# A second drain of GpSimd in the last turn but one of a routed-attention and expert kernel

## The chip, the cores and the metric

The kernel runs on one core of one Trainium2 chip. A core has five engines with an instruction stream each: TensorE (PE, with its weight loads as PEld), VectorE (DVE), ScalarE (ACT), GpSimd (POOL) and SyncE (SP). They meet through semaphores. The metric is the device time of one execution in microseconds, and a kernel's time is the median of several executions.

## What is computed

There are two blocks, one behind the other. The first is attention in which a query attends only to the keys of its own cluster: `q`, `k` and `v` are 4 x 8 x 768 x 64, and each head has 16 centroids.

```python
q_assign = argmax(q_n @ c_n);  k_assign = argmax(k_n @ c_n)
mask = q_assign[:, :, :, None] == k_assign[:, :, None, :]
attn = softmax(where(mask, q @ k.T / sqrt(64), -1e9));  x = attn @ v
```

The result is seen as 3072 tokens (rows) of 512 columns. The second block sends each token to one of 8 experts, the one with the largest logit, and weighs the expert's answer by the softmax probability of that expert:

```python
e = argmax(x @ w_gate);  gate = softmax(x @ w_gate)[e]
y = gate * (relu(x @ w1[e]) @ w2[e])        # w1: 512 x 1024, w2: 1024 x 512
```

All is float32. No token is dropped, so the number of tokens of an expert follows from the data.

## The kernel before

**Attention.** Sixteen pairs of heads are worked through in turn: scores on TensorE, exponentials on ScalarE, sums on VectorE. The finished rows are stored to a DRAM buffer, `x_rows`. For each of the four batches `number(b)` works out a place for every token in a DRAM list sorted by expert, and writes the list with GpSimd: six indirect DMAs per batch (L541), 24 in all.

**Turns.** The expert block then runs in ten turns, `s` = 0 to 9. A turn takes up to a fixed number of tokens of one expert: 288 and 288 in the two early turns, then 256, 288, 288, 384, 416, 416, 448 and 128. The expert of a turn is read at run time from a small table. For each turn GpSimd gathers the token rows, 128 at a time, with indirect DMAs (`gather`, L672, 30 in all). VectorE weighs and transposes them, `layer1` multiplies by `w1`, `layer2` by `w2`, and `write` (L976 and L977) scatters each finished tile of up to 128 rows to `out` with one indirect DMA of GpSimd (30 in all). A finished tile is in a `z` buffer, of which there are three.

**The order of the work.** The schedule is written by hand: each engine's instructions run in the order in which the Python code emits them. Work for later turns is put between the steps of the present one with hooks: `at(h1, i, f, ...)` has `f` called at the i-th hook of the turn's first layer, `at(h2, i, f, ...)` at the i-th of the second. `layer1` has a hook behind each of its seven products in each of two halves, so that hook 4 comes in the first half, behind the fifth product. In turn 8 (448 tokens) that hook calls one sum of `w2` blocks for VectorE. Turn 8 has no gather of its own to issue, because `s + 2` is beyond the last turn; what stands in GpSimd's stream from there on is the four scatters of turn 8 and the one of turn 9.

**The end.** Behind the last turn each engine reads a flag (L1173) and branches over a general path that these inputs don't need (L1174). Then the program is closed on leaving the context of L1435, where SP waits for the outstanding semaphores in turn, every engine runs a drain instruction and they meet at a barrier. That code is not in the kernel's text; the drain of GpSimd in it is the first in its stream since the start of the program, where another stands (L1426).

Of the kernel before, what the change touches and what calls it, by code (L numbers as in the profile page):

```python
# [33 lines left out]
def kernel(  # L34
# [11 lines left out]
    nc = tc.nc  # L46
# [116 lines left out]
    with tc.manual_schedule(), ExitStack() as actx:  # L163
# [476 lines left out]
        def places(s):  # L640
            g = GR[s]
            off = nc.sync.value_load(xe[0:1, NS + s : NS + s + 1], min_val=0, max_val=(E - 1) * NPL + N)
            T = g["T"]
            full, rem = divmod(T, P)
            sf = g["sf"] = xp.tile([P, NJ, TR], F32, name="sf", bufs=4)
            nc.sync.dma_start(
                out=sf[:, 0:full, :], in_=t_d[bass.ds(off, full * P), :].rearrange("(j p) o -> p j o", p=P)
            )
            if rem:
                nc.sync.dma_start(out=sf[0:rem, full, :], in_=t_d[bass.ds(off + full * P, rem), :])  # L650
# [48 lines left out]
        def take(s):  # L699

            g = GR[s]
            T, C = g["T"], g["C"]
            g["xs"] = xp.tile([P, T_MAX // Q4, P], F32, name="xs")
            for r in range(HP):
                nc.sync.dma_start(
                    out=g["xs"][Q4 * r : Q4 * (r + 1), 0:C, :],
                    in_=g_d[s][0:T, P * r : P * (r + 1)].rearrange("(c t) d -> t c d", t=Q4),
                )
# [60 lines left out]
        for b in range(B - 1):  # L769
            n = HP * (b + 1)  # L770
            last = b == B - 2
# [56 lines left out]
    with tc.manual_schedule(), ExitStack() as ectx:  # L828
# [125 lines left out]
        def pairs_of(s):  # L954


            return GR[s]["T"] // (2 * P) if s else 0

        def h_sums(s):

            g = GR[s]
            g["H"] = []
            for p in range(pairs_of(s)):
                c0 = 2 * P * p
                h = g["h"]
                a11, a21 = h[:, 0:4, c0 : c0 + P], h[:, 0:4, c0 + P : c0 + 2 * P]
                a12, a22 = h[:, 4:8, c0 : c0 + P], h[:, 4:8, c0 + P : c0 + 2 * P]
                t = [hpool.tile([P, 4, P], F32, name=f"hs{i}") for i in range(4)]
                V = nc.vector
                strassen(V, t[2], a11, a21, ALU.subtract)  # L970
                strassen(V, t[0], a21, a22, ALU.add)
                strassen(V, t[1], t[0], a11, ALU.subtract)
                strassen(V, t[3], a12, t[1], ALU.subtract)
                g["H"].append((a11, a12, a22, t))
# [113 lines left out]
        last = NS - 1  # L1088

        def first_weights(s):  # L1090
            if s >= len(EARLY):
                expert(s)
            GR[s]["w1"] = fetch1(GR[s]["e"], (wa, wb)[s % 2])

        def second_weights(s):
            GR[s]["w2"] = fetch2(GR[s]["e"], (wa, wb)[s % 2])

        for s in range(NS):
            h1, h2 = {}, {}

            def at(d, i, f, *a):
                d.setdefault(i, []).append(lambda: f(*a))

            if s == 0:
                at(h1, 2, sum_up, n - 1)
                at(h1, 2, weights_of, n - 1)
                at(h1, 3, gate, B - 1)
                at(h1, 3, gate_exp, B - 1)
                at(h1, 5, gate_sum, B - 1)
                at(h1, 5, choose, B - 1)  # L1110
                at(h1, 8, count, B - 1)
                at(h1, 9, number, B - 1)
                at(h1, 11, rows, n - 1)
                at(h1, 11, store, n - 1)
                at(h1, 12, rank_all)
                at(h2, 0, rank_rest)
                at(h2, 3, places, 2)
                at(h2, 7, indices, 2)
                at(h2, 7, gather, 2)
            if s == 3:  # L1120
                at(h1, 5, ask)
                at(h1, 9, answer)
            if s < last:
                if 2 < s + 2 <= last:
                    places(s + 2)
                if s == 0:
                    first_weights(1)
                elif s > 1:
                    take(s + 1)
                if s == 1:  # L1130
                    at(h1, 6, weigh, 2)
                    at(h1, 7, take, 2)

                    at(h1, 7, first_weights, 2)
                    at(h1, 8, second_weights, 2)
                else:
                    second_weights(s + 1)
                if 0 < s <= last - 2:
                    at(h2, 0, first_weights, s + 2)

                if s == 0:
                    when = ((h2, 1), (h2, 2), (h2, 4), (h2, 5), (h2, 7), (h2, 7))
                elif s == 1:
                    when = ((h2, 2), (h2, 3), (h2, 4), (h2, 5), (h2, 6), (h2, 6))
                else:
                    when = ((h1, 9), (h1, 10), (h2, 1), (h2, 2), (h2, 2), (h2, 5))
                if GR[s + 1]["T"] >= 2 * P:
                    for (h, i), f, a in zip(when, (w1_sums,) * 4 + (w2_sums,) * 2, (2, 1, 0, 3, 2, 0)):
                        at(h, i, f, s + 1, (a,), nc.vector)
                at(h2, 1 if s == 1 else 3, turn_rows, s + 1)  # L1150
                if GR[s + 1]["T"] >= 2 * P:
                    at(h2, 1 if s == 1 else 4, x_sums, s + 1)
            if s == 0:
                at(h1, 2, gather, 1)
                at(h1, 8, weigh, 1, slice(0, 1))
                at(h1, 11, weigh, 1, slice(1, 2))
                at(h1, 12, weigh, 1, slice(2, 3))
                at(h1, 12, take, 1)
            elif s + 2 <= last:
                at(h1, 5 if s == 2 else 4, indices, s + 2)  # L1160
                at(h1, 5 if s == 2 else 4, gather, s + 2)
                at(h2, 6 if s == 1 else 4, weigh, s + 2)
            if pairs_of(s):
                at(h1, 4, w2_sums, s, (1,), nc.vector)
                at(h1, 6, w2_sums, s, (3,), nc.vector)
            (layer1 if GR[s]["T"] >= 2 * P else few_columns)(s, h1)
            h_sums(s)
            layer2(s, h2)
# [271 lines left out]
```

## Time and profile before

| what | value |
| --- | --- |
| median of 3 runs | 679.32 us (677.63 to 682.28) |
| the profiled execution's own time | 680.02 us |
| its span in the profile | 678.2 us |
| TensorE busy | 648.1 us, 96% of the span |
| VectorE, ScalarE busy | 512.5 and 301.0 us |
| GpSimd busy, instructions | 124.4 us, 145 |
| indirect DMAs of GpSimd | 84 (24 at L541, 30 at L672, 30 at L977) |

The profile is of one execution, whose time is the span and 1.8 us that lie outside it. All times inside it count from the start of the span. Instructions that the sequencer handles alone, such as branches, semaphore waits and drains, don't count as busy; they are found under the line that they belong to, with a q behind the engine's name (POOLq, SPq). A GpSimd DMA's duration is the time of its issue, not that of its data. The time that the page puts down as idle before an instruction is time of that engine, and costs something only where the end depends on it.

### The profile page before, as it was taken

The numbers are of one execution on the slowest core, as the hardware profiler recorded it, in microseconds if no ns is written. First come the engines' busy times: TensorE is split into PE (matmuls) and PEld (weight loads), VectorE is DVE, ScalarE is ACT, GpSimd is POOL, SyncE is SP. The second block draws the span as 40 slices with busy tenths as digits, with TensorE's granted clock in tenths as the row PEclk, the third lists the DMA queues.
The fourth block names the chain that finished last, engine by engine and source line by source line (L and its number), as shares of the span: only waits on it lengthen the run. The fifth ranks groups of instructions, "written<-read, shape, count | busy, mean of one in ns | idle before, by whom it ended". The sixth has DMA issues, their size and how long they took to land.

```text
span 678.2 us, 11364 instructions
## 1 busy us (share of the span) xinstructions
PE 648.1 (96%) x4210; PEld 424.3 (63%) x4210; DVE 512.5 (76%) x909; ACT 301.0 (44%) x524; POOL 124.4 (18%) x145
## 2 busy tenths in 40 slices
PE   4999999999999999999999989999999999999993
PEld 2445444455444454444484879978797977869771
DVE  5889999999999999999887788886868375562300
ACT  2756556667556566556432323333231332413210
POOL 4000000012000300222113522324241422040010
PEclk9899999999999999999999989999999999999997
DMA  9723455433455434356473498667494837523010
GB/s 185 144 51 73 88 94 94 67 70 69 80 94 94 73 73 78 63 152 197 113 264 96 147 388 281 227 261 251 196 288 175 271 127 218 201 73 135 7 49 17
DMA packets 191807, 95.37 MB, mean 141 GB/s; under 512 B 155967, under 2 KB 173887, under 8 KB 190464
## 3 DMA queue, kind: packets, MB, share of 16 engines
q1 hardware_dynamic: 184016, 81.12, 43.8%
q0 software_dynamic: 4928, 12.97, 5.8%
q10 hardware_dynamic: 2800, 0.48, 0.4%
q8 instruction: 35, 0.57, 0.4%
q14 instruction: 28, 0.23, 0.1%
HBM read 74.10 MB, written 20.70 MB: 140 GB/s over the span
## 4 chain that ended last, share of the span: by engine, by line
PE 52%; issue 27%; DVE 8%; DMA 5%; POOL 5%; SPq 2%; ACT 1%; POOLq 0%; DVEq 0%; ACTq 0%
PE sps L370 19%; PE mps L395 15%; PE bank L902 4%; PE bank L1003 3%; PE sbank L902 3%; POOL out_dram L977 3%; PE sbank L1003 2%; PE mps L415 2%; PE bank L1022 2%; PE mps L304 2%; DVE acc L389 2%; POOL xg L672 1%; DMA w<-in_moe_w_dram 1%; DVE a L723 1%; DVE xw L689 1%
## 5 line engine op out<-in xcount | busy, mean ns | idle before, releaser
L383 ACT ACTIVATE A<-sps 128x768 f32<-128x768 f32 x192 | 153.1, 811 | 47.3 <-PE sps L370 46.2
L370 PE MATMUL sps<-qT,kT 64*128 64x384 f32 x768 | 160.2, 496 | 1.9 <-ACT A L383 1.9
L389 DVE TENSOR_TENSOR acc<-acc,A 128x768 f32<-128x768 f32 x128 | 121.4, 948 | 9.7 <-ACT A L383 3.3
L395 PE MATMUL mps<-A,v_in 128*64 128x384 f32 x768 | 127.4, 488 | 0.0
L370 PEld LDWEIGHTS sps<-qT,kT 64*128 64x128 f32 x768 | 66.8, 188 | 57.8 <-issue 51.0
L395 PEld LDWEIGHTS mps<-A,v_in 128*64 128x64 f32 x768 | 53.8, 137 | 70.5 <-issue 62.2
L977 POOL DMA_INDIRECT out_dram<-z,si x30 | 47.8, 1594 | 199.9 <-DVE z L860 170.7
L541 POOL DMA_INDIRECT tokens_of<-tg,pos_i x24 | 27.1, 1128 | 291.8 <-DVE pos_i L539 145.8
L370 PE MATMUL sps<-mq,mk 64*128 64x384 bf16 x384 | 63.4, 324 | 2.7 <-ACT mq L350 2.7
L1022 PE MATMUL bank<-w,h 128*128 128x512 f32 (+2 forms) x224 | 64.4, 596 | 0.0
L672 POOL DMA_INDIRECT xg<-x_rows,gi x30 | 41.4, 1382 | 50.7 <-DVE gi L662 19.3
L350 ACT COPY mq<-ohT 32x384 bf16<-32x384 bf16 x64 | 32.6, 510 | 38.7 <-DVE ohT L340 29.5
L902 PE MATMUL sbank<-xc,a 128*128 128x144 f32 (+4 forms) x288 | 48.0, 310 | 1.4 <-ACT h L920 0.7
L902 PE MATMUL bank<-xT,w 128*128 128x144 f32 (+4 forms) x288 | 47.8, 309 | 0.0
L902 PEld LDWEIGHTS bank<-xT,w 128*128 128x128 f32 x288 | 43.9, 191 | 2.6 <-issue 2.2
L1022 PEld LDWEIGHTS bank<-w,h 128*128 128x128 f32 (+2 forms) x224 | 24.6, 151 | 32.5 <-issue 32.3
L902 PEld LDWEIGHTS sbank<-xc,a 128*128 128x128 f32 x288 | 43.3, 190 | 2.1 <-issue 1.2
L860 DVE TENSOR_TENSOR h<-sbank,p 128x288 f32<-128x288 f32 (+4 forms) x18 | 9.2, 513 | 46.8 <-PE sbank L902 45.7
L370 PEld LDWEIGHTS <-mk 64*128 64x128 bf16 x384 | 19.5, 94 | 28.2 <-DVE mk L352 3.3
L920 ACT ACTIVATE h<-h 128x288 f32<-128x288 f32 (+4 forms) x36 | 17.6, 488 | 41.4 <-DVE h L860 32.6
L689 DVE TENSOR_TENSOR xw<-xg,sf 128x256 f32<-128x256 f32 (+2 forms) x60 | 32.8, 607 | 2.2 <-DMA xg<-x_rows,gi 1.7
L389 DVE TENSOR_TENSOR acc<-A 128x768 f32<-128x768 f32 x32 | 30.3, 947 | 5.1 <-ACT A L383 5.0
(205 smaller groups left out, 884.5 us busy)
## 6 DMA issues: line engine op xcount, KB each, us to landing
w<-in_moe_w_dram SPq DMA_DIRECT2D x20, 2048.0 KB
v_in<-in_v_dram SPq DMA_DIRECT2D x32, 192.0 KB
x_rows<-x SPq DMA_DIRECT2D x64, 96.0 KB
turn_rows<-xw SPq DMA_DIRECT2D x23, 256.0 KB
q_in<-in_q_dram SPq DMA_DIRECT2D x60, 96.0 KB
k_in<-in_k_dram SPq DMA_DIRECT2D x60, 96.0 KB
xs<-turn_rows SPq DMA_DIRECT2D x16, 144.0 KB
xs<-turn_rows SPq DMA_DIRECT2D x8, 208.0 KB
```

The source lines that it names most:

```text
L350: nc.scalar.copy(dst, src)
L370: nc.tensor.matmul(SP[n, h, j][:, a, 0:HS], lhsT=kt[rows, j * P : (j + 1) * P], rhs=qt[rows, h * HS : (h + 1) * HS], start=first, stop=not ...
L383: nc.scalar.activation(A[n, h, j], ps[:, :, 0:HS], AF.Exp, scale=D**-0.5)
L389: nc.vector.tensor_tensor(ACC[n, h], first, A[n, h, j], op=ALU.add)
L395: nc.tensor.matmul(O[n, h][D * a : D * (a + 1), 0:HS], lhsT=VIN[n][:, a, j, :], rhs=A[n, h, j][:, a, :], start=(j == 0), stop=(j == NQ - 1),)
L541: ins = nc.gpsimd.indirect_dma_start(out=t_d[:, :], out_offset=bass.IndirectOffsetOnAxis(ap=pos_i[:, i : i + 1], axis=0), in_=tg[:, b, i, ...
L672: nc.gpsimd.indirect_dma_start(out=xg[0:m], out_offset=None, in_=x_d[0:rows_in, :], in_offset=bass.IndirectOffsetOnAxis(ap=g["gi"][0:m, j ...
L689: nc.vector.tensor_tensor(xw[0:m, :, :, d2 * a : d2 * (a + 1)], xg[0:m].rearrange("p (r a d b) -> p a r b d", r=HP, a=2, b=DB)[:, a], g["s ...
L902: nc.tensor.matmul(ps[:, f * T2 : (f + 1) * T2], lhsT=w[:, k, (2 * j + f) * P : (2 * j + f + 1) * P], rhs=x[:, k, :], start=first and f + ...
L977: ins = nc.gpsimd.indirect_dma_start(out=out[:, :], out_offset=bass.IndirectOffsetOnAxis(ap=GR[s]["si"][0:rows, j : j + 1], axis=0), in_=z ...
L1003: nc.tensor.matmul(ps[:, 0:H], lhsT=x[:, k, :], rhs=y[:, k, :], start=first and k == 0, stop=k == 3, skip_group_check=not first,)
L1022: nc.tensor.matmul(ps[i * m : (i + 1) * m, :], lhsT=h[:, f, j * P : j * P + m], rhs=w[:, f, :], start=(k == 0), stop=(k == FB // n - 1),)
```

## The change

One call is added in the loop over turns. In turn 8 (`last` is 9) the hook that calls the sum of `w2` blocks now also emits a drain instruction on GpSimd. In GpSimd's stream it stands behind the scatter of turn 7's last tile and ahead of the scatter of turn 8's first.

```diff
             if pairs_of(s):
                 at(h1, 4, w2_sums, s, (1,), nc.vector)
                 at(h1, 6, w2_sums, s, (3,), nc.vector)
+            if s == last - 1:
+
+                at(h1, 4, nc.gpsimd.drain)
             (layer1 if GR[s]["T"] >= 2 * P else few_columns)(s, h1)
             h_sums(s)
             layer2(s, h2)
```

## The prediction

> **What bounds the kernel now.** I read the head of the page first (what is busy), then GpSimd's timeline over the last turns (what stands around the added instruction), and last the instructions of the kernel's closing line, L1435, because the chain of waits stops short of them.
>
> The head of the page:
> ```profile
> span 678.2 us, 11364 instructions
> PE 648.1 (96%) x4210; PEld 424.3 (63%) x4210; DVE 512.5 (76%) x909; ACT 301.0 (44%) x524; POOL 124.4 (18%) x145
> ```
> TensorE is busy for 96% of the span, so nearly all of the kernel is a matmul stream that an instruction of GpSimd can't shorten. GpSimd is busy for 18%. What isn't TensorE is mostly at the two ends.
>
> GpSimd from the last scatters of turn 7 on (start, duration, line, what it does, how long it sat idle before and for what):
> ```profile
> 605.63 0.98 POOL L977 DMA_INDIRECT out_dram<-z,si  x1 [0.30 <-issue]
> 609.50 0.97 POOL L977 DMA_INDIRECT out_dram<-z,si  x1 [2.89 <-ACT z L1029]
> 636.72 0.93 POOL L977 DMA_INDIRECT out_dram<-z,si  x1 [26.25 <-DVE z L860]
> 644.74 0.98 POOL L977 DMA_INDIRECT out_dram<-z,si  x1 [7.09 <-DVE z L860]
> 646.34 0.97 POOL L977 DMA_INDIRECT out_dram<-z,si  x1 [0.63 <-ACT z L1076]
> 653.42 0.97 POOL L977 DMA_INDIRECT out_dram<-z,si  x1 [6.11 <-ACT z L1029]
> 667.43 0.97 POOL L977 DMA_INDIRECT out_dram<-z,si  x1 [13.04 <-ACT z L1029]
> ```
> The scatter at 609.50 is turn 7's last, the one at 636.72 turn 8's first. Between them GpSimd idles for 26.25 us. After 667.43 nothing is issued that moves data, and yet the span lasts to 678.2.
>
> Stages of that tail (start to end, its length, busy time of PE, PEld, DVE, ACT and POOL, then clock, DMA share, GB/s):
> ```profile
> 669.40:670.40 1.00, 0.00 (x0) 0.00 (x0) 0.00 (x0) 0.00 (x0) 0.00 (x0) 1.00 0.21 78
> 670.40:671.50 1.10, 0.00 (x0) 0.00 (x0) 0.00 (x0) 0.00 (x0) 0.00 (x0) 0.55 0.00 0
> 671.50:677.40 5.90, 0.00 (x0) 0.00 (x0) 0.00 (x0) 0.00 (x0) 0.00 (x0) 0.50 0.00 0
> ```
> The last scatter's data are through by 670.4. For 7 us no engine computes and nothing moves. Who is late is in the instructions of L1435, those that touch 671.0 to 677.3 (engine's queue, operation, count, shortest/median/longest ns, first and last start):
> ```profile
> L1435 SPq EVENT_SEMAPHORE  x7: 27/28/28, 671.0 to 671.3; - x7
> L1435 SPq DRAIN  x2: 7/10/13, 671.4 to 671.5; - x2
> L1435 POOLq DRAIN  x1: 6934/6934/6934, 670.4 to 670.4; - x1
> ```
> and over the whole kernel:
> ```profile
> L1435 POOLq DRAIN  x3: 46/107/6934, 670.4 to 677.9; - x3
> L1435 DVEq DRAIN  x2: 10/14/17, 648.9 to 677.7; - x2
> L1435 ACTq DRAIN  x2: 8/8/8, 667.8 to 677.7; - x2
> ```
> One drain of GpSimd runs 6.934 us, from 670.45 to 677.38. SP, the last of the others, has arrived at 671.48. The end of the kernel is therefore set by that drain alone, 5.9 us after everyone else.
>
> **What the Trainium skill says.** "Perfetto Trace Analysis", section "Per-engine timelines", states that for an instruction of the sequencer alone, DRAIN among them, the reported window is execution and not the wait for semaphores. So the 6.934 us should be work, not a wait on another engine, and the silent DMA engines agree. "VectorE: DVE Perf Modes", section "The DRAIN you can't avoid", calls the drains around a kernel some 12 ns, constant, on all five engines. The trace agrees for the others (7 to 17 ns) and not for GpSimd (46, 107, 194 and 6934 ns); the measurement decides. "DMA: Bandwidth & Descriptors", section "SWDGE vs HWDGE vs iDMA", says that for a DMA issued from GpSimd a software core computes the descriptors and appends them to rings. No page that I found says what GpSimd's drain does with those rings.
>
> **The price of the long drain.** GpSimd's other drains are free of it: 194 ns at the start, before any of its DMAs, and 107 and 46 ns after the long one. So it isn't a fixed price of the instruction; it goes with DMAs issued since the previous drain. By the page GpSimd issues 24 + 30 + 30 = 84 indirect DMAs (L541, L672, L977). SP's wait for the last landing starts at 670.36 and takes 333 ns, to 670.69, so at most 0.24 us of the drain can be that landing. The rest is 677.38 - 670.69 = 6.69 us, and by 84 **80 ns per DMA**, if each is settled in turn. That is an estimate: the trace has no second drain with DMAs before it.
>
> **The change, part by part.** It removes nothing and moves nothing. It issues no DMA and passes no queue of SP. It adds one instruction on GpSimd, at the fifth hook of turn 8's first layer, behind 79 of the 84 DMAs.
>
> *The new drain.* It can start at 610.48. Turn 7's last scatter has its last packet 6.5 us after its issue (609.50), at 616.0 by the DMA packets. Settling 79 DMAs costs 79 x 0.080 = 6.3 us. One after the other it ends at 622.3; if it settles early ones while it waits, sooner. The bounds are 610.7 (0.19 us, a drain with nothing to do) and 616.0 + 6.9 = 622.9. Behind it on GpSimd is only the scatter of 636.72, so its cover is GpSimd's 26.25 us idle gap, with 13.8 us left even at the upper end. I cost it at **nothing**. Without the cover it would cost its own length, but only past the z buffers' slack, worked out under the slower rival. If it gets a wait of its own at that hook, for the VectorE sum listed ahead of it (at 618.51 at the latest in that part of the turn), it ends near 626 and is hidden still.
>
> *The final drain.* Five DMAs remain: 5 x 0.080 = 0.4 us, with 0.05 to 0.19 us for an empty drain. After the landing at 670.69 it ends between 671.1 and 671.3. The bounds are 670.7 (nothing left) and 677.4 (the price unchanged). The saving can't be taken in full, because **SP is late next**: its chain of semaphore waits, from 670.69 on, ends with its drain at 671.48. GpSimd, which collects the arrivals, goes on some 0.04 us later, at 671.52, where it now goes on at 677.43. The saving is 677.43 - 671.52 = **5.9 us**. The 0.8 us of barrier and clearing after it stays.
>
> *Side effects.* Scatters issued after the new drain might be dearer or cheaper for the software; a first one after a pause has taken 1.65 us and a later one 0.97. Only the issue at 667.43 lies on the end's path, and it stands 31 us behind the first. I take 0, with 0.7 us either way for the range.
>
> Sum: 680.02 us for the profiled execution (span 678.2 plus 1.8 outside it) less 5.9 gives 674.1. The median of the three runs shown is 679.32, 0.7 below that execution; the same saving gives **673.4 us**, a ratio of 0.991.
>
> **The rivals.**
> - *The final drain keeps its price* (679.3). It could settle rings or the end of the program and not DMAs, say 16 DMA engines at 0.43 us each, or depend on a state that the first drain doesn't clear. For it: 6.9 us divides as well by 16, and one long drain can't show how it scales. Against it: the two drains that follow it take 0.1 us. The new drain would then be long and hidden, the last one long and bare.
> - *A partial effect* (676 to 678): a settled entry is still looked at, at a fraction of the price, or the price sits with the last DMAs. Each 10% of the 6.7 us that stays is 0.7 us, after a free 0.2. Nothing speaks for it but that scaling is unseen. I count it with the first rival.
> - *Slower: the new drain outlasts its cover.* The place is GpSimd's gap before 636.72. Turn 8 uses three z buffers, so the copy of its last tile (done at 653.4) needs the buffer whose scatter is issued at 646.34. With about 1.3 us for each scatter issued back to back and 2.4 us to land, the three before it have to begin by some 647. The drain delays the kernel from a length of about 37 us on (610.5 to 647), over five times the longest one measured. A length of 50 us, less the 5.9 saved, gives 679.3 + 13 - 5.9 = 686. For it speaks only that its real length in mid-kernel is unmeasured.
> - *The instruction has no effect* (679.3): if it lands elsewhere in GpSimd's stream, for instance before most of the DMAs. The records of drains would show that; I count it with the first rival.
>
> **How the numbers follow.** The forecast, a mid-kernel drain that empties the final one, gets 0.85, the unchanged or partial cases 0.12, the slower one 0.03. The three runs lie between 677.6 and 682.3, so 1% is about what a measurement of this kernel can tell from no change, and 0.87% lies just under it. I split the forecast's 0.85 into 0.36 over 1% (the base may be nearer the profiled 680, the residue smaller, the runs luckier) and 0.49 within; with the rivals that is 0.36 faster, 0.61 within 1%, 0.03 slower. The range is the forecast with 2.4 us of spread below, like the runs' own, and above up to 677.5 to take in part of the partial case. All cases of weight have one sign or none.
>
> **What would show it.** In the changed profile: a long drain of GpSimd between 610 and 623 (the step "6.3 us"); a final drain under 1 us; GpSimd's barrier following SP's drain by some 0.04 us; the scatters at 636.7 to 667.4 where they are; a tail from the last scatter's issue of 4.9 us in place of 10.8. I am wrong if the final drain stays near 6.9 us, if the mid one is short, or if the scatter of 636.7 waits for it.

## The result, and the profile after

The changed kernel takes 673.21 us (median of 6 runs, 671.3 to 674.09) beside 678.8 us for the kernel before (median of 6, 677.47 to 682.28). The ratio is **0.9901, 95% interval 0.9882 to 0.9921**, so it is about 1% faster. This ratio is an estimate of its own and not the quotient of the two medians, which lie 5.6 us (0.8%) apart; the same holds for the ratios below. The profiled execution took 672.78 us, its span is 671.1.

The head of the page after:
```profile
span 671.1 us, 11365 instructions
PE 648.0 (97%) x4210; PEld 424.2 (63%) x4210; DVE 512.5 (76%) x909; ACT 301.6 (45%) x524; POOL 123.5 (18%) x145
```
No engine has less to do: TensorE is busy for 648.0 us, as it was for 648.1. The gain lies where no engine was busy.

GpSimd from the last scatters of turn 7 on, after (columns as in the view of before):
```profile
608.34 0.97 POOL L977 DMA_INDIRECT out_dram<-z,si  x1 [2.91 <-ACT z L1029]
635.56 0.93 POOL L977 DMA_INDIRECT out_dram<-z,si  x1 [26.25 <-DVE z L860]
...
666.27 0.97 POOL L977 DMA_INDIRECT out_dram<-z,si  x1 [13.04 <-ACT z L1029]
```
The idle gap ahead of turn 8's first scatter is 26.25 us, to the last digit what it was. The new drain is in it, under the line that calls the hook (engine's queue, operation, count, shortest/median/longest ns, first and last start):
```profile
L1102 POOLq DRAIN  x1: 11247/11247/11247, 608.1 to 608.1; - x1
```
It runs from 608.11 to 619.35, and 16 us of the gap are left. The drain at the end, which belongs to L1438 now, with SP's instructions beside it:
```profile
L1438 SPq EVENT_SEMAPHORE  x14: 17/28/1839, 667.6 to 671.0; - x14
L1438 POOLq EVENT_SEMAPHORE  x4: 17/17/17, 670.3 to 670.9; - x4
L1438 POOLq DRAIN  x3: 46/107/1969, 667.7 to 670.8; - x3
L1438 SPq DRAIN  x3: 7/7/13, 670.2 to 670.5; - x3
```
The final drain takes 1.969 us in place of 6.934, from 667.71 to 669.68. Most of that is waiting: the semaphore of the last landing comes at 669.44, and the drain ends 0.25 us behind it. (A landing is the arrival of a DMA's data; its time is that of the DMA's last semaphore update in the trace.) SP's wait of 1839 ns is for the same landing; SP arrives at 670.24, later than GpSimd, whose first semaphore instruction behind it starts at 670.3. So SP sets the end now. From the issue of the last scatter to the end of the span it is 4.8 us (666.27 to 671.1), where it was 10.8. These 6.0 us are the change's effect. The other 1.2 us between the two spans came before the last scatter, which in the profiles of kernels with the same work ahead of it starts anywhere between 664.9 and 667.8.

A second instruction of the end became shorter as well, one that the prediction left out. It is INC_SWDGE_SEM, an instruction of GpSimd's sequencer ahead of the final drain, of which the runs show the time and not the purpose. Before:
```profile
L1174 POOLq INC_SWDGE_SEM  x1: 1872/1872/1872, 668.5 to 668.5; - x1
```
and after:
```profile
L1177 POOLq INC_SWDGE_SEM  x1: 293/293/293, 667.4 to 667.4; - x1
```
Before, it stood on the path of the end, because the final drain follows it on GpSimd at once (670.42 to 670.45). The last landing came 0.22 us after the drain's start and didn't hold it up: the experiments show that half of a drain can run while a landing is awaited. So the end cost GpSimd 1.87 us and 6.93 us before. The shorter INC_SWDGE_SEM adds nothing of its own to the gain, since SP is last now: with 1.87 us still ahead of it the short drain would end near 669.7 (an estimate from the figures above), and SP arrives at 670.24.

### The profile page after: what moved, and what is told of

Its sections match the earlier page's. It is cut to its first block, busy times and chain, and to the rows that moved or that the text cites. A ratio compares the mean times of both kernels' runs of the same rounds, so it can differ in the third digit from the quotient of the medians.

```text
span 671.1 us, 11365 instructions
## 1 busy us (share of the span) xinstructions
PE 648.0 (97%) x4210; PEld 424.2 (63%) x4210; DVE 512.5 (76%) x909; ACT 301.6 (45%) x524; POOL 123.5 (18%) x145
## 3 DMA queue, kind: packets, MB, share of 16 engines
q0 software_dynamic: 4928, 12.97, 5.8%
## 4 chain that ended last, share of the span: by engine, by line
PE 56%; issue 26%; DMA 5%; POOL 5%; DVE 4%; SPq 1%; ACT 1%; POOLq 0%; DVEq 0%
PE sps L370 21%; PE mps L395 16%; PE bank L902 4%; PE bank L1003 4%; PE sbank L902 3%; PE sbank L1003 3%; POOL out_dram L977 2%; DMA w<-in_moe_w_dram 2%; PE mps L415 2%; PE mps L304 2%; PE bank L1022 2%; POOL xg L672 1%; DMA xg<-x_rows,gi 1%; DVE xw L689 1%; DVE acc L389 1%
```

## The experiments

Each experiment's edit is against the changed kernel, or against the one before where the text says so. All keep the whole computation. "The tail" is the time from the issue of the last scatter to the end of the span: 10.78 us before, 4.78 after.

**The change again**, timed beside the last of the experiments.

> The changed kernel itself, as the measure for the run beside it: 673, ratio to before 0.990.

It took 673.75 us beside 679.19 for the kernel before, ratio 0.9918 (0.9896 to 0.9939), with an added drain ("middle drain" from here on) of 11.470 us and a tail of 4.68 us. The result stands.

**How does the price grow with the DMAs left?** The added drain is moved to an earlier turn. With `s == 4` 28 DMAs are left to the final drain, with `s == 1` 46.

```diff
-            if s == last - 1:
+            if s == 4:
 
                 at(h1, 4, nc.gpsimd.drain)
```

> The one added drain stands in turn 4, behind 56 of the 84 DMAs of GpSimd, so 28 are left to the final drain. If 80 ns per DMA is all paid behind the last landing, the final drain ends 2.2 us behind it and the kernel is 4.5 us faster than before. If the price falls into two passes, one of some 38 ns per DMA that can run while a landing is awaited and one of some 42 ns behind it, the final drain ends 1.2 us behind the landing and the saving is 5.5 us. If the price goes with packets and not with DMAs, about the same (28 DMAs are scatters and gathers with most of the packets), 3 us or less. If the final drain has a fixed price, no saving.

It took 673.02 us beside 679.07, ratio 0.9915 (0.9887 to 0.9944). The tail is 5.23 us, 5.55 less than before: the two passes' 5.5 and not the single price's 4.5. The final drain of this kernel, in a window around it:
```profile
L1438 POOLq DRAIN  x1: 2487/2487/2487, 667.9 to 667.9; - x1
```
It starts 1.3 us ahead of the last landing and ends 1.19 us behind it, which is 28 x 42 ns. The median lies 6.05 us under that of before, more than the tail's 5.55, but the start of the last scatter varies by more than this difference.

> The added drain stands in turn 1, 46 DMAs are left to the final drain. One price of 80 ns behind the landing: it ends 3.7 us behind it, saving 3.0 us. Two passes: 1.8 us for the first, of which about 1 lies ahead of the landing, 1.9 for the second, end 2.7 us behind the landing, saving 4.0 us. Price by packets: nearly all packets are still ahead, saving under 2 us. Fixed price: none.

It took 675.26 us, ratio 0.9938 (0.9924 to 0.9952). The tail is 6.91 us, 3.87 less than before (4.0 expected of two passes, 3.0 of one price).
```profile
L1438 POOLq DRAIN  x3: 46/107/3812, 667.2 to 671.5; - x3
L1177 POOLq INC_SWDGE_SEM  x1: 1112/1112/1112, 666.0 to 666.0; - x1
```
46 DMAs cost 3.812 us, 82.9 ns each, where 84 cost 6.934, 82.5 each. And INC_SWDGE_SEM follows them too: 293 ns for 5, 752 for 28, 1112 for 46, 1872 for 84, which is 193 ns and 20 ns per DMA. A fixed price of the final drain is out. This drain began 0.96 us ahead of its landing and is no longer per DMA for it: a landing that came while the first pass still ran cost nothing.

**Is it the DMAs, or what they move?** To the kernel before, without the added drain, 42 small DMAs of GpSimd are added in its idle stretch during attention.

```diff
+        more = consts.tile([16, 42, 4], F32, name="more")
+
+        def more_dmas():
+            for i in range(42):
+                nc.gpsimd.dma_start(out=more[:, i, :], in_=v[0, 0, 16 * i : 16 * i + 16, 0:4])
+
+        at_pair(7, 3, more_dmas)
```

> The kernel before, without the added drain, with 42 more DMAs of GpSimd, each of 16 rows of 16 bytes, in its long idle stretch during attention (from 165 us on). Price per DMA: the final drain grows from 6.9 to 10.3 us and the kernel is 3.4 us slower than before, or 4.2 if the semaphore instruction ahead of it grows too and isn't hidden any more. Price by packets (42 x 16 or so on 4928, 14%): 7.9 us, 1 us slower. Price by bytes (10 KB on 13 MB) or fixed: 6.9 us, no change.

The final drain, and SP's instructions, in a window that starts behind the last landing:
```profile
L1443 SPq DRAIN  x2: 7/10/13, 676.2 to 676.3; - x2
L1443 POOLq DRAIN  x1: 10364/10364/10364, 675.7 to 675.7; - x1
```
and, from the view of the line ahead of it:
```profile
L1182 POOLq INC_SWDGE_SEM  x1: 2727/2727/2727, 672.9 to 672.9; - x1
```
The drain grew to 10.364 us: by 126 DMAs 82.3 ns each. GpSimd's queue moved 6272 packets in place of 4928 (27% more, not the 14% that I had set down), which would have given 8.8 us, and next to no more bytes. The time since the previous drain is nearly the same, 675 us and 670. So the price goes with the number of DMAs, and the small plain ones cost as much as the large indirect ones. It starts 3.1 us behind the last landing here, so none of it is waiting.

The kernel took 687.99 us beside 679.46, ratio 1.0116 (1.0078 to 1.0154): 8.5 us slower, not 3.4 to 4.2. The tail is 17.36 us, 6.58 more than before. Of that the drain is 3.43 and INC_SWDGE_SEM 0.86, together 4.3 us, where 4.2 were expected at most. The other 2.3 us lie behind GpSimd's branch at the end: from its start to the next instruction it is 2.80 us (669.8 to 672.6), before 0.50 (667.78 to 668.28). The last scatter is 2.1 us later as well, and why is open, as is the branch's delay. The trace has three packets of an instruction queue (q14) behind the last scatter, here and in the next run, and two in every run without the 42 DMAs; whether the branch waited for instructions the runs don't show.

**Both together:** the 42 DMAs and the added drain in turn 8.

> The same 42 DMAs, with the added drain in turn 8. Price per DMA, paid once: the middle drain is longer than 11.2 us by 42 x 42 to 42 x 80 ns (1.8 to 3.4), all hidden; the final drain ends as in the changed kernel, and so does the kernel, 673. If the final drain looks at older DMAs again, slower than the changed kernel by 1 us or more.

The middle drain took 11.824 us, only 0.6 more than the 11.247 of the changed kernel, where 1.8 to 3.4 were expected: its landing came sooner. The one at the end:
```profile
L1446 POOLq DRAIN  x3: 46/103/466, 673.7 to 674.8; - x3
```
So the 121 DMAs ahead of the middle drain are gone from the final one. The middle drain ends 5.00 us behind its landing, in the changed kernel 3.28: 41.3 and 41.5 ns by the DMAs ahead. The kernel took 676.67 us, ratio 0.9951 (0.9934 to 0.9968), and not 673. Its tail is 5.27 us, 0.5 longer for the late branch. The rest is the last scatter's start, at 669.83, later than in any kernel without the 42 DMAs. That they cost something before the end is likely, with two kernels that have them; the runs don't show where.

**Is a drain counted twice?** Two drains one behind the other.

```diff
                 at(h1, 4, nc.gpsimd.drain)
+                at(h1, 4, nc.gpsimd.drain)
```

> Two drains one behind the other at the place of the change. If a drain settles what was issued since the last one, the second takes 0.05 to 0.2 us and the final drain is unchanged at about 2 us; time as the changed kernel, 673. If a drain looks at all DMAs of the program each time, the second takes 3 to 7 us, still hidden, and the final one would be long too. If it has a fixed price, the second takes 6.7 us.

```profile
L1102 POOLq DRAIN  x2: 47/5162/10277, 609.6 to 619.9; - x2
```
The second takes 47 ns. A drain settles what was issued since the last one, and nothing twice. The kernel took 674.34 us, ratio 0.9914 (0.9881 to 0.9946), tail 4.94.

**Does the hook matter?** The same drain at a later hook of the same layer.

```diff
-                at(h1, 4, nc.gpsimd.drain)
+                at(h1, 12, nc.gpsimd.drain)
```

> The added drain stands at hook 12 of turn 8's first layer in place of hook 4; GpSimd's stream is the same as in the changed kernel, so its time should be the same (673). If the sequencer starts it at once behind the scatter, its length is again some 11.2 us with the landing in it. Nothing tells the theories apart here except that a hook further on brings no wait of its own.

GpSimd's stream is the same, and the drain starts 58.17 us ahead of the last scatter's issue, as in the changed kernel. It takes 10.163 us, less than the 11.2 expected because the landing came sooner, and ends 3.28 us behind its landing. The kernel took 671.87 us, ratio 0.9904 (0.9865 to 0.9944). The hook places it in GpSimd's stream and nowhere else.

**Is it the cover?** To the kernel before, a drain behind the last scatter, with nothing to hide it.

```diff
             layer2(s, h2)
+        nc.gpsimd.drain()
 
     jobs.close()
```

> The added drain stands behind the last scatter, with nothing left to hide it. If the cover is what makes it free: this drain ends about 6.7 us behind the last landing like the final one of before, the final one then takes 0.2 us or less, and the time is that of before within 1 us (679). If a second drain by itself shortened the end: near 673.

The added drain and then those of the closing line:
```profile
L1169 POOLq DRAIN  x1: 8145/8145/8145, 666.5 to 666.5; - x1
L1436 POOLq DRAIN  x3: 34/51/107, 676.2 to 677.5; - x3
```
The final drain has nothing left (51 ns), and yet the time is 679.6 us, ratio **1.0000 (0.9988 to 1.0011)**. The drain took the 84 DMAs' full price in either place; what the change gains is that it lies beside turn 8's matmuls. That the ratio is so exactly 1 is chance in part. With no INC_SWDGE_SEM ahead of it the added drain ends 7.9 us behind the last scatter's issue, where the final drain of before ended 9.9 behind it; but GpSimd's reading of the flag, its branch and SP's chain come behind it now, and the tail is 11.05 us beside 10.78. It ends 5.2 us behind the last landing, not the expected 6.7, because it runs from the end of the issue on: 84 DMAs in 6.94 us, with the landing 1.7 us after their start.

**Must the cover be an idle gap?** The drain in turn 8's second layer, between two scatters that follow each other closely.

```diff
-                at(h1, 4, nc.gpsimd.drain)
+                at(h2, 5, nc.gpsimd.drain)
```

> The one added drain stands in turn 8's second layer, between the scatters of z1 and z0, where GpSimd has no idle gap: the next scatter comes 1.6 us behind the last. With the two passes that the first runs fit (41 ns per DMA each, 81 DMAs) it takes some 6.7 us from the end of the z1 issue, so z0's scatter starts near 651.4 in place of 645.2, its data land 2.4 us later, and the copy of turn 8's last tile, which needs that z buffer, starts 2.7 us late; behind it on ScalarE are the relus of turn 9. The last scatter is 2 to 3 us later than in the changed kernel and the time 675 to 676, still 3 us under before, since the final drain is short. If a drain in mid-kernel is cheap where no landing is awaited, 673. If its delay passes on in full, 679 to 680.

It took 674.05 us, ratio 0.9930 (0.9913 to 0.9946), beside 0.9918 for the changed kernel in the same comparison: no measurable difference. GpSimd, and then ScalarE's copy of the turn's last tile:
```profile
643.30 0.97 POOL L977 DMA_INDIRECT out_dram<-z,si  x1 [7.09 <-DVE z L860]
651.84 0.97 POOL L977 DMA_INDIRECT out_dram<-z,si  x1 [7.56 <-ACT z L1029]
653.12 0.97 POOL L977 DMA_INDIRECT out_dram<-z,si  x1 [0.30 <-issue]
```
```profile
651.13 0.59 ACT L1029 COPY z<-bank 128x512 f32<-128x512 f32 x1 [6.49 <-PE bank L1022]
```
The drain takes 7.903 us, and the next scatter is issued 8.5 us behind the last one, in place of 1.6. The length was right, its consequence wrong. The copy starts at 651.13, ahead of the late scatter, as soon as its bank is ready. So it doesn't need the buffer that this scatter still has to read, and nobody waits for it. Which buffer it takes the trace doesn't name.

**Who is late next?** The drain in turn 9, so that one DMA is left.

```diff
-            if s == last - 1:
+            if s == last:
 
-                at(h1, 4, nc.gpsimd.drain)
+                at(h1, 2, nc.gpsimd.drain)
```

> The added drain stands in turn 9, behind 83 of 84 DMAs, so one is left. If SP's chain of waits is what is late next, the time is that of the changed kernel (673, within 0.5 us), although four DMAs fewer are left to the final drain. If the final drain still set the end, 0.2 to 0.3 us faster. The drain has 13 us of idle time there and should end near 661, ahead of the last scatter; if it is longer than 13 us, the last scatter waits and the kernel is slower than the changed one by what is over.

It took 672.19 us, ratio 0.9874 (0.9840 to 0.9909), which overlaps with the changed kernel's interval. The tail is 4.84 us beside 4.78: with four DMAs fewer it is no shorter, as SP's chain lets expect:
```profile
L1438 POOLq DRAIN  x3: 46/107/1960, 667.3 to 670.6; - x3
L1438 SPq DRAIN  x3: 7/7/13, 670.0 to 670.3; - x3
```
The final drain ends at 669.30, 0.08 us behind the last landing, and SP arrives at 670.02. The middle drain ends at 659.81, 6.2 us ahead of the last scatter. None of the places tried is measurably better than that of the change.

## Why the prediction was right

- **What bounds the end.** Right. The final drain alone held the end, 5.9 us behind SP. With it short, SP is last, as predicted, at 3.96 us behind the last scatter's issue in place of the 4.04 of before. The prediction left out INC_SWDGE_SEM ahead of the drain: its 1.87 us were on the same path.
- **The price, 80 ns per DMA, paid once.** Right in kind and nearly in size: 82.5 ns by 84 DMAs, 82.3 by 126. I had taken 0.24 us off for the landing, and none of the drain was waiting: its price per DMA is the same in the run with 126, which starts 3.1 us behind its landing. That it isn't fixed was argued from the empty drains behind it (107 and 46 ns); the series 5, 46, 84 and 126 shows it.
- **That the drain's record is work and no wait**, after "Perfetto Trace Analysis", section "Per-engine timelines". Right for the 6.934 us, and not in general: of the middle drain's 11.247 us 7.96 had passed when the last landing's semaphore came. The page leaves the wait for semaphores out of the record; what GpSimd's drain awaits of its own DMAs stands inside it.
- **The new drain, 6.3 us behind the landing, end at 622.3.** Its length was off, inside the bounds given. It ends 3.28 us behind its landing in each of three other runs with the same 79 DMAs ahead, too. The prediction's 622.3 had the whole price paid behind the landing, and it left open that early DMAs are settled while it waits. Half is paid in either: the lengths fit two passes of some 41 ns per DMA, of which the first runs while a landing is awaited. Every drain whose first pass was over when its landing came ends 0.04 us and 41 ns per DMA behind it: 0.08 us for 1, 0.25 for 5, 1.19 for 28, 1.61 for 38 and 2.34 for 56 (the middle drains of the two runs with 46 and 28 left), 3.28 for 79, 5.00 for 121. What the passes do the runs don't show.
- **Its cover.** Right: 16 us of the gap are left. The slower rival's reckoning with the z buffers, that the copy of turn 8's last tile needs the buffer of the scatter at 646.34, was wrong: with that scatter 7 us late nothing waited. How late turn 8's first scatter may be wasn't tried.
- **The final drain, 0.4 us and the price of an empty one.** It ends 0.25 us behind the landing, for the same reason: five DMAs' second pass. The sign "a final drain under 1 us" did not come, at 1.969 us: INC_SWDGE_SEM had shrunk too, so the drain began 1.7 us ahead of the landing and waited for it.
- **The saving, 5.9 us.** The tail became 6.0 us shorter, the medians 5.6 apart, with 673.21 us measured for 673.4 predicted. The saving rests on the right mechanism, SP's arrival; that the time fits to 0.2 us is luck, as single runs of the changed kernel lie up to 2.8 us apart. On which side of 1% the change lies stays open, as it did in the forecast: the ratio's interval, 0.9882 to 0.9921, takes in both.
- **The rivals.** A final drain that keeps its price, or part of it, is out by the series; a drain that outlasts its cover by the measured lengths. The drain behind all scatters shows that without cover the price is merely moved.

## What to carry to other kernels

Read the closing line's instructions when the span goes on behind the last data: a drain of GpSimd at the end may be settling every DMA that GpSimd issued in the whole kernel, here 82 ns each. One drain of GpSimd late in the kernel, beside other engines' work, takes that off the end; past the point where SP is late next, an exact place is worth nothing. SP arrives 0.80 us behind the last landing here, so by the figures above up to some 18 DMAs could be left to the final drain for free; that is an estimate, with no run between 5 and 28. Without such a drain, fewer DMAs issued by GpSimd should shorten the end at the same price; that is not shown, only that more of them lengthen it.

## What the runs showed that I had not expected

- GpSimd's INC_SWDGE_SEM ahead of the final drain costs 193 ns and 20 ns per DMA since the last drain, to 2.727 us for 126 of them. With the drain's 82 ns it is some 102 ns per DMA, of which the 20 ns and the drain's first pass can hide behind the last landing and the second pass can't.
- A drain's record can begin before the issue of the DMA ahead of it ends: the one at 608.11 starts before the scatter at 608.34. Where no landing holds it up its length is 1.21 us and 82.6 ns per DMA (8.065 us for 83, 7.903 for 81, 8.145 for 84). The 1.21 us are the time until that issue ends.
- 42 small DMAs of GpSimd in an idle stretch made the kernel 8.5 us slower, twice what their settling costs at its end (4.3 us). The rest is not explained.
